# Attention with v's adds: sign turns of queries' and keys' rounded values, and the adding transfers behind them, placed 4 to 11 half-steps later

## The chip, the core and the metric

One core of a Trainium2 chip runs the whole program. The metric is device microseconds from start to end, as the median of several executions of one compiled kernel. A profile of one execution shows where its time lies.

## What is computed

Attention in which a query sees only the keys of its own hash bucket (six sign bits of a projection), then a mixture of experts on its output. Cut to what matters:

```python
q_bits = einsum('bhsd,dk->bhsk', q, proj) > 0        # k_bits likewise, 6 bits
mask   = q_bucket[:, :, :, None] == k_bucket[:, :, None, :]
scores = where(mask, q @ k.T / sqrt(D), -1e9)
attn   = exp(scores - rowmax); attn /= attn.sum(-1) + 1e-9
x      = (attn @ v) as rows of 512                    # 4 batches, 8 heads, 768 rows, 64 wide
out    = moe(x, w_gate, w1, w2)                       # 8 experts, capacity rows/8
```

Queries and keys are fp32. To multiply them with fp16 matmuls and keep fp32's precision, each is used as a rounded fp16 value and an fp16 remainder ("high" and "low").

## The kernel before, in words

Attention works on 32 heads in 8 groups of four. A head has six steps, each of two half-steps, so a group is 48 half-steps and the program lists its work by half-step. A step computes scores for one block of 128 keys (lines 322 and 323, into `pst`), ScalarE's exp (line 324, into `pt`), the rounding remainder of `pt` on GpSimd or VectorE (`lo`, lines 328 and 331), the products with v four steps later (lines 345 to 347), and about one pass that finds row maxima for a later head (lines 273 and 275). Once in 12 half-steps, so once a head, ScalarE turns a head's maxima (line 290, `mr`) and lays them into `qa` with a small DMA (line 293). These rows of line 290 are called marks below.

Group G needs its high and low parts in the layout of the matmuls (`qa`, `qb`, `ka`, `kb`, two buffers each). The road there, for G from 4 to 7, in half-steps before the group's first one (`P4`, `Z4`):

- SyncE loads `qp` and `kp` (fp32) from memory.
- ScalarE casts them to `qh` and `kh` (fp16) in eight pieces (line 149), from half-step -35 to -15.
- ScalarE writes the negative of the rounded value into `ql` and `kl` in four pieces: the sign turns (`turn`, line 153).
- GpSimd issues two adding DMAs (`adds`, line 155), each of which adds the fp32 original from memory to `ql` or `kl`, so that the remainder stands there.
- SyncE's queue then moves `qh`, `kh`, the sign bits, and last `kl` and `ql` into the matmul buffers (`moves`, lines 182 to 216), in a fixed order from half-step -47 on, that is from +1 of the group before.

`qh`, `kh`, `ql`, `kl`, `qp` and `kp` have one buffer each. So the first turn of group G writes `ql` only when the move of the group before it out of `ql` (`qb<-ql`, line 200, the last of that group's moves) has landed. Instructions of one engine run in the order in which they were written: a ScalarE instruction that waits holds every exp behind it, and the score matmuls write into three `pst` buffers that the exps must empty.

The lines that place them:

```python
def turn(G,w,p):
    A.activation(TMP[G,'l'][w][:,p],TMP[G,'h'][w][:,p],AF.Copy,scale=-1.0)
def adds(G,w):
    G_.dma_start(TMP[G,'l'][w]...,(qT,kT)[w][G]...,accum_op=ALU.add)
...
z=AP['Z3'] if G==3 else [48*(G-1)+x for x in AP['Z4']]
add(z[n],turn,G,n%2,n//2)        # n=0..3: q pair 0, k pair 0, q pair 1, k pair 1
if n<2: add(z[4+n],adds,G,n)     # q, k
```

v goes a like way inside the group before: cast (line 218), turn (line 223) and an adding DMA (`vl`, line 227) at half-step +25, and TensorE sums `vh` and `vl` at +33 (line 237).

Of the kernel before, what the change touches and what calls it, by code (L numbers as in the profile page):

```python
# [41 lines left out]
 TV=1,  # L42
 AV=[5,7],
 Z3=[77,85,88,91,93,97],
 Z4=[-31,-19,-25,-13,-19,-11],
 EA=[262, 32, 5],
 EG={2: 0, 3: 3},
 MO=['', 'AKs', 'BqL', 'lmk', 'c|ABqKLslmk', 'ABqKLs|cklm', 'ABqKLs|cklm'],
# [9 lines left out]
def attention(tc, nc, ctx, qT, kT, vv, proj, wg, x_dram, L, jp, identf, ident, B, late=None, after=None):  # L58
# [349 lines left out]
    def add(n,f,*a):  # L408
        if n>=2*(6*NH+LAG+6): raise ValueError('an operation has no step')
        at.setdefault(n,[]).append((f,a))  # L410
# [15 lines left out]
    for G in range(1,NG):  # L426
# [5 lines left out]
        for n in range(4):  # L432
            if G<3: add(p[8+n],sub,G,n%2,n//2)
            else:
                z=AP['Z3'] if G==3 else [48*(G-1)+x for x in AP['Z4']]
                add(z[n],turn,G,n%2,n//2)
# [621 lines left out]
```

## Time and profile before

| | |
|---|---|
| median of 3 runs | 742.94 us (741.41 to 744.52) |
| profiled execution | 742.8 us, of which the span is 740.9 us |
| TensorE busy in the span | 660.6 us, 89% |
| VectorE, GpSimd, ScalarE busy | 522.3, 508.9, 399.6 us |

Attention ends at about 410 us; the experts follow. Busy shares are means over stages with different limits, so the table says which engine is busiest and not what a change is worth: that is read from the stretch in which the change stands.

### The profile page before, as it was taken

Reading aid. Unit: us, or ns where it says so; the run is one execution under the profiler, and the core shown is the slowest. Engines: PE = TensorE matmul, PEld = TensorE weight load, DVE = VectorE, ACT = ScalarE, POOL = GpSimd, SP = SyncE. Lnnn points to the kernel's source line nnn. Section 1 sums busy time; section 2 is a strip of 40 time slices with the busy share of each in tenths; the row PEclk is TensorE's granted clock in tenths of the full one; section 3 lists DMA queues with packets and bytes.
Section 4 is the critical chain, followed back from the end, with each engine's and each line's share of the span. In section 5 each row is a group of like instructions: output and inputs, shape, how many; then the busy total and the mean of one; then the engine's idle time right before and its main releaser. Section 6 shows DMA issues by size and latency. Waiting matters only on the chain. (4 is left out here: it accounts for less than half of the span.)

```text
span 740.9 us, 19022 instructions
## 1 busy us (share of the span) xinstructions
PE 660.6 (89%) x7761; PEld 424.5 (57%) x7769; DVE 522.3 (70%) x1220; ACT 399.6 (54%) x821; POOL 508.9 (69%) x469
## 2 busy tenths in 40 slices
PE   8999999499589598699999669999999999999994
PEld 2666666277357366467777556555555555555551
DVE  7879889178388387389788774989878888843120
ACT  6876886467557556657557125443434344444530
POOL 7899987378558577476884054585787878797761
PEclk9999999699899899899999759999999999999998
DMA  8649778668685686676322153526170708072601
GB/s 214 195 112 198 178 180 165 135 107 175 137 145 141 131 153 162 117 159 144 33 52 66 32 157 115 191 108 237 77 282 31 282 33 284 31 284 88 239 30 42
DMA packets 65020, 104.51 MB, mean 141 GB/s; under 512 B 29040, under 2 KB 53668, under 8 KB 62884
## 3 DMA queue, kind: packets, MB, share of 16 engines
q1 hardware_dynamic: 55236, 51.10, 29.1%
q0 software_dynamic: 8944, 52.04, 24.9%
q8 instruction: 61, 1.00, 0.6%
q10 hardware_dynamic: 752, 0.15, 0.1%
q14 instruction: 27, 0.22, 0.1%
HBM read 71.32 MB, written 12.58 MB: 113 GB/s over the span
## 5 line engine op out<-in xcount | busy, mean ns | idle before, releaser
L328 POOL TENSOR_TENSOR lo<-pt 128x768 f16<-128x768 f32 x148 | 243.0, 1675 | 95.0 <-ACT pt L324 90.5
L275 DVE TENSOR_REDUCE m<-pss 128x1 f16<-128x770 f32 x192 | 181.4, 956 | 81.0 <-PE pss L273 79.9
L324 ACT ACTIVATE pt<-pst 128x384 f32<-128x384 f32 x384 | 172.4, 490 | 88.4 <-PE pst L323 81.3
L322 PE MATMUL pst<-qa,ka 128*128 128x384 f16 x384 | 127.6, 333 | 39.6 <-ACT pt L324 36.4
L345 PE MATMUL psv<-vh,pt 128*128 128x65 f16 x1152 | 126.9, 196 | 1.6 <-DVE X L363 1.6
L323 PE MATMUL pst<-qb,kb 128*128 128x384 f16 x384 | 127.5, 333 | 0.0
L347 PE MATMUL psv<-vh,lo 128*128 128x65 f16 x1152 | 126.6, 196 | 0.7 <-POOL lo L328 0.5
L346 PE MATMUL psv<-vl,pt 128*128 128x64 f16 x1152 | 126.8, 195 | 0.0
L345 PEld LDWEIGHTS <-pt 128*128 128x128 bf16 x1152 | 108.7, 99 | 18.9 <-issue 4.5
L346 PEld LDWEIGHTS <-pt 128*128 128x128 bf16 x1152 | 107.5, 100 | 11.8 <-issue 1.2
L347 PEld LDWEIGHTS <-lo 128*128 128x128 f16 x1152 | 107.4, 99 | 1.1 <-POOL lo L328 0.8
L875 ACT CAST wh<-wf 128x1024 f16<-128x1024 f32 x64 | 65.4, 1042 | 75.2 <-DMA wf<-in_w_dram,zwidx 46.6
L273 PE MATMUL pss<-ka,qa 128*128 128x385 f16 x384 | 96.2, 335 | 6.5 <-DVE m L275 5.6
L887 POOL TENSOR_TENSOR wl<-wf,wh 128x512 bf16<-128x512 f32 x74 | 84.1, 1152 | 0.0
L323 PEld LDWEIGHTS <-kb 128*128 128x128 f16 x384 | 37.9, 99 | 61.8 <-issue 41.4
L910 PEld LDWEIGHTS <-wh 128*128 128x128 f16 x544 | 50.7, 99 | 31.1 <-issue 1.4
L866 POOL DMA_INDIRECT wf<-in_w_dram,zwidx x20 | 19.6, 981 | 57.2 <-DVE zmi L799 30.6
L910 PE MATMUL ph<-xx,wh 128*128 128x384 f16 (+1 forms) x304 | 57.3, 315 | 0.3 <-issue 0.3
L922 PEld LDWEIGHTS <-hh 128*128 128x128 f16 x384 | 35.5, 98 | 36.3
L322 PEld LDWEIGHTS <-ka 128*128 128x128 f16 x384 | 38.2, 99 | 27.2 <-issue 2.8
L910 PE MATMUL po<-xx,wh 128*128 128x384 f16 x240 | 48.1, 326 | 0.0
L997 POOL TENSOR_TENSOR wl<-wf,wh 128x512 bf16<-128x512 f32 x36 | 42.6, 1211 | 4.4 <-ACT wh L875 4.3
(294 smaller groups left out, 1221.7 us busy)
## 6 DMA issues: line engine op xcount, KB each, us to landing
vp<-in_vv_dram SPq DMA_DIRECT2D x8, 768.0 KB
x_dram<-XS SPq DMA_DIRECT2D x16, 384.0 KB
qp<-in_qT_dram SPq DMA_DIRECT2D x7, 768.0 KB
kp<-in_kT_dram SPq DMA_DIRECT2D x7, 768.0 KB
qa<-qh SPq DMA_DIRECT2D x14, 192.0 KB
ka<-kh SPq DMA_DIRECT2D x14, 192.0 KB
qb<-qh SPq DMA_DIRECT2D x14, 192.0 KB
kb<-kh SPq DMA_DIRECT2D x14, 192.0 KB
```

Of the source, the lines that this page charges most:

```text
L273: T.matmul(ps[:,hf,0:HK],QA[u][:,j,qc*128:qc*128+128],KA[u][:,j,hf*HK:hf*HK+HK],start=True,stop=True)
L275: V.tensor_reduce(M6[h][:,qc:qc+1],ps[:,:,0:HK],axis=AX.XY,op=ALU.max,negate=True)
L322: T.matmul(ps[:,0:384],KA[u][:,j,kr],QA[u][:,j,r],start=True,stop=False)
L323: T.matmul(ps[:,0:384],KB[u][:,j,kr],QB[u][:,j,r],start=False,stop=True)
L324: A.activation(PT[h,kc][0][:,r],ps[:,0:384],AF.Exp,scale=0.125)
L328: eng.tensor_tensor(l,p,p.bitcast(BF)[:,1::2],op=ALU.subtract)
L345: T.matmul(av[:,c,:],ph[:,r],VH[u][:,j,kc,:],start=(kc==0 and c==0),stop=False,skip_group_check=True)
L346: T.matmul(av[:,c,0:64],ph[:,r],VL[u][:,j,kc,:],start=False,stop=False,skip_group_check=True)
L347: T.matmul(av[:,c,:],l[:,r],VH[u][:,j,kc,:],start=False,stop=False,skip_group_check=True)
L875: s.nc.scalar.copy(h[:,r],f[:,r])
L887: for _ in range(n): s.nc.gpsimd.tensor_tensor(*s.pend.pop(0)[1],op=ALU.subtract)
L910: T.matmul(p[:,r],a[:,o:o+128],b[:,d,r],start=n==0 and not c,stop=n==11 and c in (None,2),skip_group_check=c is not None)
```

## The change

One row of the table of positions: for groups 4 to 7 the turns move from half-steps -31, -19, -25, -13 (q pair 0, k pair 0, q pair 1, k pair 1) to -20, -12, -18, -9, the adds of q from -19 to -15 and those of k from -11 to -6. Group 3 has its own row, `Z3`, which stays. Nothing is computed that was not computed before.

```diff
- Z4=[-31,-19,-25,-13,-19,-11],
+ Z4=[-20,-12,-18,-9,-15,-6],
```

On ScalarE, ahead of group 5 and right behind the casts of v, this stood before (`vl` and `vh` are v's low and high parts, line 324 is the exp):

```order
L218 CAST vh_215<-vp 128x6x64
L153 ACTIVATE ql<-qh 128x768
L324 ACTIVATE pt<-pst 128x384
L223 ACTIVATE vl_216<-vp 128x384
L218 CAST vh_215<-vp 128x6x64
L324 ACTIVATE pt<-pst 128x384
L223 ACTIVATE vl_216<-vp 128x384
L149 CAST qh<-qp 128x384
L324 ACTIVATE pt<-pst 128x384 x2
L149 CAST qh<-qp 128x384
L324 ACTIVATE pt<-pst 128x384 x2
L153 ACTIVATE ql<-qh 128x768
```

Now both turns of q stand behind the next mark, and the first meets `qb<-ql` there:

```order
L149 CAST kh<-kp 128x384
L324 ACTIVATE pt<-pst 128x384
L290 ACTIVATE mr<-pst,mb_198,ms_199 24x128
L324 ACTIVATE pt<-pst 128x384
L149 CAST kh<-kp 128x384
L293 DMA qa_171<-mr 4x6x128
L324 ACTIVATE pt<-pst 128x384
L153 ACTIVATE ql<-qh 128x768
L324 ACTIVATE pt<-pst 128x384 x2
L153 ACTIVATE ql<-qh 128x768
```

The first turn has gone from ahead of the casts of q's second pair to behind two casts of k; the mark, the casts and the exps keep their order.

On GpSimd, which issues the adds between its `lo` instructions (line 328), the same stretch read before:

```order
L227 DMA vl_216<-in_vv_dram 128x1536
L558 IOTA wt_88 128x8
L328 TENSOR_TENSOR lo<-pt 128x768 x2
L155 DMA ql<-in_qT_dram 128x1536
L585 TENSOR_SCALAR wt<-wt_88 128x8
L586 TENSOR_SCALAR wtb<-wt_88 128x8
L328 TENSOR_TENSOR lo<-pt 128x768 x2
L155 DMA kl<-in_kT_dram 128x1536
```

and reads now:

```order
L227 DMA vl_216<-in_vv_dram 128x1536
L558 IOTA wt_88 128x8
L328 TENSOR_TENSOR lo<-pt 128x768 x2
L585 TENSOR_SCALAR wt<-wt_88 128x8
L155 DMA ql<-in_qT_dram 128x1536
L586 TENSOR_SCALAR wtb<-wt_88 128x8
L328 TENSOR_TENSOR lo<-pt 128x768 x2
L562 MEMSET tiny 128x1
L328 TENSOR_TENSOR lo<-pt 128x768 x2
L155 DMA kl<-in_kT_dram 128x1536
```

The add of q passes one small instruction, the add of k two `lo` and one small one. SyncE's and TensorE's orders are as before.

## Rows read from the trace of the kernel before

**Rows 1.** The page: busy us, share of the span, instructions of each engine.
```profile
PE 660.6 (89%) x7761; PEld 424.5 (57%) x7769; DVE 522.3 (70%) x1220; ACT 399.6 (54%) x821; POOL 508.9 (69%) x469
```

**Rows 2.** Waits (us in total, times, longest), 140:340, then whole span.
```profile
PE pst L322 <- ACT pt L324: 35.8, 4, 10.3
...
ACT ql L153 <- DMA qb<-ql: 31.3, 4, 8.7
```

**Rows 3.** ScalarE's timeline at the four waits: start, us, [idle <-releaser].
```profile
139.56 0.84 ACT L153 ACTIVATE ql<-qh 128x768 f16<-128x768 f16 x1 [8.73 <-DMA qb<-ql]
...
193.37 0.84 ACT L153 ACTIVATE ql<-qh 128x768 f16<-128x768 f16 x1 [7.65 <-DMA qb<-ql]
...
248.58 0.84 ACT L153 ACTIVATE ql<-qh 128x768 f16<-128x768 f16 x1 [7.30 <-DMA qb<-ql]
...
302.40 0.84 ACT L153 ACTIVATE ql<-qh 128x768 f16<-128x768 f16 x1 [7.63 <-DMA qb<-ql]
```

**Rows 4.** TensorE's timeline at the second wait, same columns.
```profile
194.64 0.48 PE L322 MATMUL pst<-qa,ka 128*128 128x384 f16 x1 [8.62 <-ACT pt L324]
...
196.86 0.53 PE L322 MATMUL pst<-qa,ka 128*128 128x384 f16 x1
...
198.95 0.33 PE L322 MATMUL pst<-qa,ka 128*128 128x384 f16 x1
```

**Rows 5.** SyncE's timeline at the second wait.
```profile
184.85 0.45 SPq L78 DMA_DIRECT2D kp<-in_kT_dram  x1
...
187.62 1.76 SPq L200 DMA_DIRECT2D qb<-ql  x2
```

**Rows 6.** Busy time by stretch: one burst, then mark to mark (L290).
```profile
core 0: us, PE busy (x) PEld busy (x) DVE busy (x) ACT busy (x) POOL busy (x), PEclk, DMA share, GB/s
185.00:195.00 10.00, 1.39 (x9) 0.68 (x7) 2.44 (x5) 2.35 (x6) 1.86 (x3) 0.81 1.00 237
125.72:148.81 23.09, 12.42 (x154) 8.43 (x150) 8.01 (x12) 11.87 (x28) 10.83 (x11) 0.70 0.60 116
181.64:201.39 19.75, 11.13 (x157) 7.83 (x154) 8.60 (x12) 11.82 (x28) 10.70 (x12) 0.83 0.52 125
237.06:256.30 19.24, 10.84 (x157) 7.74 (x154) 8.59 (x12) 11.73 (x29) 10.28 (x11) 0.82 0.59 126
290.75:310.52 19.77, 11.23 (x157) 7.85 (x154) 7.77 (x12) 11.77 (x29) 9.57 (x11) 0.83 0.59 124
343.00:352.90 9.90, 9.56 (x157) 6.94 (x154) 9.80 (x13) 8.54 (x23) 6.98 (x5) 1.00 0.74 163
201.39:212.70 11.31, 10.78 (x162) 8.01 (x159) 8.82 (x13) 9.15 (x22) 9.07 (x10) 1.00 0.83 141
160.70:172.25 11.55, 11.37 (x176) 7.49 (x174) 9.57 (x16) 5.69 (x15) 11.07 (x10) 1.00 0.93 152
212.70:227.68 14.98, 12.83 (x176) 8.52 (x174) 12.67 (x14) 5.98 (x18) 9.25 (x7) 0.89 0.66 120
```

**Rows 7.** DMA issues: 384 KB adds, median us to landing.
```profile
ql<-in_qT_dram POOLq DMA_DIRECT2D x5, 384.0 KB, 8.8
...
vl<-in_vv_dram POOLq DMA_DIRECT2D x5, 384.0 KB, 6.4
```

**Rows 8.** GpSimd's timeline: adds of k, group 3, then 4.
```profile
111.51 1.21 POOL L155 DMA_DIRECT2D kl<-in_kT_dram  x1
...
161.15 0.86 POOL L155 DMA_DIRECT2D kl<-in_kT_dram  x1
```

**Rows 9.** DMA queue of the adds, 160 to 168 us: share of 16 engines.
```profile
q0 software_dynamic: 144, 0.39, 47.4%
```

**Rows 10.** Waits for DMAs, 100 to 420 us: total, times, longest.
```profile
PE pst L237 <- DMA vl<-in_vv_dram: 1.6, 3, 0.7
...
ACT qh L149 <- DMA qp<-in_qT_dram: 0.3, 1, 0.3
```

**Rows 11.** VectorE's line 373: min/median/max ns.
```profile
L373 DVE TENSOR_TENSOR XS<-X,XS x15: 944/1350/4867, 58.2 to 402.5; 128x768 f16<-128x768 f32 x15
```

## What the change will do, predicted from the trace of the kernel before

> **What bounds the kernel now.** I read the page first: TensorE is busy 89% of the span [rows 1], so time is won only where TensorE stands still. Next the waits of TensorE through the attention of the later groups: from 140 to 340 us it waited four times for an exp of line 324, 35.8 us together, the longest 10.3 us [rows 2]. Over the whole span ScalarE waited four times for the transfer `qb<-ql` ahead of line 153, 31.3 us [rows 2]. The reader is to see that these are the same four stops. ScalarE's timeline has them: turns at 139.56, 193.37, 248.58 and 302.40 us, after 8.73, 7.65, 7.30 and 7.63 us of waiting [rows 3]. TensorE's timeline shows what the second costs: it stood for 8.62 us, a moment longer than ScalarE, since the exps have to start again first, and then a score matmul took 0.53 us where 0.33 us is usual [rows 4], for the granted clock had fallen. So the place of the turn, and not an engine's work, makes these four holes.
>
> How much they cost together is read best with the marks (line 290, one in 12 half-steps) as a ruler. The four stretches that hold a stop last 23.09, 19.75, 19.24 and 19.77 us, 81.9 us together; the same stretch of the last group, which has no turns, lasts 9.90 us, with TensorE busy 9.56 us and the clock at 1.00 throughout [rows 6].
>
> **The change, part by part.** *The first turn leaves the stalled place.* It stood 3 half-steps behind a mark and now stands 14 behind it, 2 behind the next one. What is left in the four stretches? TensorE's pattern needs 9.9 us. ScalarE was busy 11.73 to 11.87 us in them [rows 6]; two turns of 0.84 us each [rows 3] are gone from there, so 10.1 us stay, just above TensorE's pace. I take 10.4 us, because such tight neighbours lose a little to each other: 4 x 10.4 = 41.6, a gain of 40.3 us. Bounds: 42.3 us at 9.9 us each, 37.5 us at 11.1 us (one more us than ScalarE's work). This gain holds the lost clock too, since the stretches are measured whole.
>
> *Where the turns go.* The next stretch had two turns and will have three: ScalarE goes from 9.15 to 10.0 us of 11.31 us. The fourth turn goes into the stretch after it, where ScalarE is busy 5.69 us of 11.55 us [rows 6]. TensorE's own work covers both; I count 0. Without that cover the four displaced 0.84 us in two stretches of each group would cost up to 6.7 us. One turn now stands ahead of the small DMA that lays maxima for a head 9 half-steps later, 0.84 us of delay against some 8 us: nothing.
>
> *A new wait at the new place.* The transfer doesn't depend on ScalarE's progress: SyncE issued `qb<-ql` from 187.62 us on, while ScalarE was standing [rows 5]. So it lands where it landed, counted from the mark ahead, at which the stretch of [rows 6] begins: turn 139.56 - 125.72 = 13.8 us at the first stop, 193.37 - 181.64 = 11.7 us at the second, 11.5 and 11.6 us at the others [rows 3, 6]. The new turn comes 14 half-steps after that mark, at 10.4 x 14/12 = 12.1 us. The first group still waits 1.7 us, the others not at all. TensorE loses about one us more than ScalarE waits (8.62 against 7.65 [rows 3, 4]): 2.7 us. Two casts of `kh` come just ahead; `kp` is issued ahead of `qb<-ql` [rows 5] and so should land no later, which makes any wait there a part of this one.
>
> *The add of k.* It moves 5 half-steps nearer to the burst in which SyncE moves `qh`, loads `qp` and moves `kh`. From 160 to 168 us, the add's own queue takes 47.4% of the 16 engines, 3.8 us of all of them [rows 9]; that work leaves a quiet place and joins a busy one. Can it make the moves late? The trace has the case: group 3's add of k was issued at 111.51 us, right at its moves, where group 4's was at 161.15 us [rows 8], and the transfer behind group 3's moves is the one that landed 13.8 us after its mark and not 11.7. So adds that stand close cost up to 2.1 us of landing. Both of group 3's stand close, here only one does, so I take half: landing 12.7 us, a wait of 0.6 us at 12.1, and with the restart some 1.0 us in three groups, 3.0 us (0 to 2.7 each). The add of q moves into a place between SyncE's bursts: 0. GpSimd holds its `lo` instructions behind an add only if the turn is late; the turns stand 3 half-steps ahead of their adds: 0.
>
> The Trainium skill ("DMA: Bandwidth & Descriptors", Queues, rings and completion order) says that a DMA engine takes turns between the queues that have work for it, packet by packet, so the add would take its share out of the burst and not wait behind it. If all 3.8 us of it came on top of the landing, the wait at the new turn would be 15.5 - 12.1 = 3.4 us in three groups, and the total 10 us worse than with the value taken; only the uncontended neighbours in the trace speak against so much.
>
> *The add of v.* It isn't moved in the program, but the stop used to end before it: now GpSimd issues it while the transfers of 185 to 195 us run, in which the DMA engines are busy through (share 1.00 [rows 6]). Alone it lands in 6.4 us; the add of q, which meets a load, takes 8.8 us [rows 7]. TensorE waits for v's add at line 237 three times even now, 1.6 us [rows 10], so there is no slack: 0 to 2.4 us each; I take the middle, 1.2 us, four times 4.8 us.
>
> *VectorE's line 373* takes 0.94 to 4.87 us [rows 11]; the long one lies in the stretch of 14.98 us, where its neighbour has 11.55 us [rows 6]. It is an encounter with GpSimd's instructions, and moving the add of k deals these cards again: 0 on the whole, 3.4 us either way for one.
>
> Sum: -40.3 + 2.7 + 3.0 + 4.8 = -29.8 us. The profiled execution took 742.8 us (span 740.9 and 1.9 around it), 0.1 us from the median of 742.94 us, so **713 us** is forecast for the median.
>
> **The rivals.**
> - *Clean:* nothing waits anew. For it: landing at 11.7 and turn at 12.1 us. Against it: the first group, and line 237 that waits already. 742.8 - 40.3 to 42.3, some 701 to 703 us.
> - *The waits form again, shorter:* the add of k delays the burst by its whole 3.8 us or by 2.1 us, the cast of `qh` waits for `qp` as it did once for 0.3 us [rows 10], the clock falls after each of these stops too. Each group would give back 5 to 8 us: 40.3 - 4 x 5 to 8 leaves 8 to 20 us, some 723 to 735 us. Against it: no row shows landing later than 13.8 us. It is the case that the Trainium skill's turn-taking (same page and section) would bring about, if the add's whole share came out of the burst; so far the trace bears out about half of it.
> - *The stop only moves:* if the transfer were tied to ScalarE, it would slip with it and the time stay at 743 us. SyncE's rows [rows 5] speak against it.
> - *Slower:* SyncE's `kb<-kl` waits for the add of k, and `qb<-ql`, transposes and v's load stand behind it in the same queue. If that add landed so late that `qb<-ql` came over 10 us later, the new wait would exceed the old one. The add is issued some 5 half-steps later, at about 165.5 us by the old clock, and would have to land after 195 us to do this, 30 us after issue; adds take 6.4 to 8.8 us [rows 7]. At 35 us it would be four times 5 us, 763 us.
>
> **How the numbers follow.** Chances: forecast (704 to 721 us) 0.58; clean (below 704) 0.16; waits again (721 to 736) 0.18; stop only moved 0.05; slower 0.03. The range leaves out half of the clean case's lower edge, the last two cases and the upper part of the third: 700 to 727 us. Less than 0.5% (3.7 us) can't be told from no change. Faster by more: 0.58 + 0.16 + 0.18 and a little of the fourth, 0.93; within: 0.04; slower: 0.03.
>
> **What would show it.** Right: the row `ACT ql L153 <- DMA qb<-ql` falls from 31.3 us to under 6, TensorE's waits of line 322 for exps from 35.8 us to under 10; the four stretches from mark to mark last 10 to 11 us with the clock at 1.00; line 237 waits 3 to 7 us for v's add. Wrong: stretches of 13 us or more (the turn or the casts wait again), longer stretches behind the second mark (the displaced turns are not covered), landing of `qb<-ql` over 14 us behind its mark (the add of k costs more than taken), or more long rows at line 373.

## The result, and the profile after

The changed kernel took 723.67 us in the median (719.88 to 732.37) where the kernel before took 742.17 us beside it: ratio 0.973, 95% interval 0.968 to 0.978. So the change gains 2.7%, about 20 us; 30 us had been forecast (713 us, with 700 to 727 us as the range). The profiled execution of the changed kernel took 719.88 us. Of its page, the line that answers to [rows 1]:

```profile
PE 657.0 (92%) x7761; PEld 421.7 (59%) x7769; DVE 525.3 (73%) x1220; ACT 398.6 (56%) x821; POOL 509.7 (71%) x469
```

TensorE's busy share rose from 89% to 92% with the same work. The waits from 100 to 375 us for TensorE, and below them two rows of the whole span (engine, line, releaser: us in total, times, longest):

```profile
PE psv L345 <- DVE X L363: 5.7, 5, 1.6
PE pst L237 <- DMA vl<-in_vv_dram: 5.0, 3, 2.6
PE pst L322 <- ACT pt L324: 3.8, 11, 0.7
PE pst L402 <- DMA XT<-XS: 2.9, 1, 2.9
...
POOL ql L155 <- ACT ql L153: 6.2, 4, 2.0
...
ACT ql L153 <- DMA qb<-ql: 0.3, 1, 0.3
```

The four stops are gone: ScalarE waits 0.3 us for `qb<-ql` where it waited 31.3 us, TensorE 3.8 us for exps where it waited some 36 us [rows 2]. Three waits of TensorE have grown beside that: for v's adding DMA at line 237 (5.0 us, before 1.6), for a quotient at line 345 (5.7 us, before 1.4), and once for a transpose at line 402 (2.9 us, before none).

The same ruler as in [rows 6], busy time from mark to mark; the first four rows are the stretches that held the stops, the next four those that follow them, the last four the ones behind these:

```profile
125.72:136.50 10.78, 9.72 (x157) 7.01 (x154) 7.76 (x12) 10.14 (x26) 8.75 (x9) 1.00 0.84 159
175.45:185.92 10.47, 9.87 (x157) 6.92 (x154) 8.59 (x12) 10.07 (x26) 10.00 (x10) 1.00 0.81 164
224.81:236.27 11.46, 10.71 (x170) 7.46 (x167) 8.95 (x13) 10.13 (x28) 10.86 (x11) 1.00 0.81 155
270.38:280.86 10.48, 9.71 (x157) 7.01 (x154) 8.08 (x12) 9.97 (x27) 9.46 (x9) 1.00 0.80 170
136.50:153.06 16.56, 13.52 (x210) 10.13 (x207) 9.17 (x14) 10.11 (x22) 8.72 (x11) 0.90 0.84 141
185.92:202.77 16.85, 13.64 (x162) 9.58 (x159) 8.93 (x13) 10.01 (x22) 8.81 (x11) 0.80 0.69 138
236.27:247.82 11.55, 11.22 (x192) 8.69 (x192) 8.96 (x13) 10.27 (x24) 7.72 (x7) 1.00 0.92 198
280.86:295.47 14.61, 12.49 (x162) 8.88 (x159) 8.93 (x13) 9.94 (x22) 7.72 (x8) 0.88 0.75 156
153.06:166.06 13.00, 11.43 (x176) 7.54 (x175) 11.58 (x16) 6.40 (x17) 11.00 (x8) 1.00 0.74 137
202.77:215.41 12.64, 11.41 (x176) 7.52 (x175) 10.98 (x14) 6.61 (x18) 10.94 (x8) 1.00 0.76 134
247.82:260.43 12.61, 11.28 (x175) 7.46 (x174) 11.00 (x14) 6.34 (x17) 10.96 (x10) 1.00 0.75 141
295.47:308.16 12.69, 11.42 (x176) 7.54 (x175) 11.09 (x14) 6.29 (x15) 10.99 (x8) 1.00 0.75 137
```

The reader is to compare three sums. The stopped stretches: 43.2 us, before 81.9 us, a gain of 38.7 us. Those behind them: 59.6 us, and before (11.93, 11.31, 11.96 and 11.32 us by the marks) 46.5 us, a loss of 13.1 us. Those behind these: 50.9 us, and before (11.51, 14.98, 11.77 and 11.77 us) 50.0 us. The last mark came at 394.4 us and comes at 368.9 us, 25.4 us earlier. From it to the end of the span were 346.5 us and are 348.9 us; the profiles of the first five runs below have 344.7 to 345.4 us there, the unaltered changed kernel among them (345.0), so these 2.4 us belong to that execution and not to the change.

What happened in the stretch of 16.85 us? GpSimd's issue of v's add, TensorE's timeline at the sums of v (start, length, [idle before <-releaser]), and below them the stretches of 2 us around the stand (the third number from the right is the granted clock):

```profile
185.52 0.88 POOL L227 DMA_DIRECT2D vl<-in_vv_dram  x1
...
191.03 0.27 PE L237 MATMUL pst<-vh,on 128*128 128x256 f16 x1 [0.38 <-ACT pt L324]
193.95 0.37 PE L237 MATMUL pst<-vl,on 128*128 128x256 f16 x1 [2.65 <-DMA vl<-in_vv_dram]
...
196.03 0.42 PE L237 MATMUL pst<-vl,on 128*128 128x256 f16 x1
...
197.25 0.83 PE L273 MATMUL pss<-ka,qa 128*128 128x385 f16 x2
```

```profile
192.00:194.00 2.00, 0.05 (x1) 0.05 (x1) 0.84 (x1) 0.15 (x1) 1.92 (x2) 0.74 1.12 360
194.00:196.00 2.00, 2.00 (x10) 1.42 (x10) 0.00 (x0) 0.00 (x0) 0.44 (x1) 0.50 0.94 132
196.00:198.00 2.00, 2.00 (x24) 1.56 (x22) 0.49 (x1) 0.88 (x2) 0.00 (x0) 0.50 0.47 61
198.00:200.00 2.00, 2.00 (x24) 1.33 (x23) 1.12 (x2) 1.09 (x3) 0.03 (x1) 0.55 0.00 0
```

It stood for 2.65 us for `vl`, and then the granted clock lay at 0.50, the lower of its two levels, until nearly 200 us: a sum took 0.42 us instead of 0.27, a pass for maxima 0.83 instead of 0.49. The stand cost 2.65 us, and the clock, by an estimate from these rows, some 3 us more: TensorE was busy throughout the six us that followed, at half its pace. The stretch of 14.61 us holds such a stand of 1.56 us at the same line. The stretch of 16.56 us is another case: there line 237 waits for no add, and the wait is that of 2.9 us for the transpose at line 402.

And in the stretches behind? VectorE's line 175, and GpSimd's timeline beside it:

```profile
207.07 1.69 DVE L175 TENSOR_SCALAR bt<-bt 128x768 f16<-128x768 f16 x1
```

```profile
206.14 0.88 POOL L155 DMA_DIRECT2D kl<-in_kT_dram  x1
206.77 1.76 POOL L328 TENSOR_TENSOR lo<-pt 128x768 f16<-128x768 f32 x1
```

Line 175 takes 0.36 us when it is undisturbed. Here it takes 1.69 us: it starts where the issue of the add of k ends (207.02 us), and it ends 0.2 us after GpSimd's next `lo` (206.77 to 208.53 us). The other three groups show the same, 1.74 to 1.79 us. The quotients behind it on VectorE come later, and that is TensorE's wait at line 345, 1.2 to 1.6 us in each of the four groups. So the row's length goes with the `lo` beside it, which the add's new place put there: in the kernel before, a row of 0.94 us with no add near it ended 0.2 us after a `lo` too. Whether the issue has a share of its own these runs don't show. It is an encounter in time and not a fixed price: in the first experiment below, with the add of k at the same half-step, the row takes 0.63 us at most, and in four of the others one of these rows takes 4.9 us (shown at the half-way turn).

### The profile page after: what moved, and what is told of

The parts are those of the page before. It is cut to its first block, busy times and chain, and to the rows that moved or that the text cites. A ratio compares the mean times of both kernels' runs of the same rounds, so it can differ in the third digit from the quotient of the medians.

```text
span 717.8 us, 19026 instructions
## 1 busy us (share of the span) xinstructions
PE 657.0 (92%) x7761; PEld 421.7 (59%) x7769; DVE 525.3 (73%) x1220; ACT 398.6 (56%) x821; POOL 509.7 (71%) x469
## 5 line engine op out<-in xcount | busy, mean ns | idle before, releaser
L322 PE MATMUL pst<-qa,ka 128*128 128x384 f16 x384 | 125.7, 328 | 7.2 <-ACT pt L324 3.8
L323 PE MATMUL pst<-qb,kb 128*128 128x384 f16 x384 | 125.6, 327 | 0.0
L273 PE MATMUL pss<-ka,qa 128*128 128x385 f16 x384 | 94.6, 330 | 5.7 <-DVE m L275 3.1
```

Source lines behind the costliest of these rows:

```text
L273: T.matmul(ps[:,hf,0:HK],QA[u][:,j,qc*128:qc*128+128],KA[u][:,j,hf*HK:hf*HK+HK],start=True,stop=True)
L322: T.matmul(ps[:,0:384],KA[u][:,j,kr],QA[u][:,j,r],start=True,stop=False)
L323: T.matmul(ps[:,0:384],KB[u][:,j,kr],QB[u][:,j,r],start=False,stop=True)
```

## The experiments

Theory A: what the changed kernel lost again, it lost at line 237, where v's add lands late, and by the clock that falls after the stand. Theory B, the rival: it lost it to the add of k and to the turns that were moved into these stretches. All ratios are to the kernel before, run on the same chip.

**Sums of v later, on the changed kernel.**

```diff
- P3=[..., 97, 111, 1, 4, 128, ...]   P4=[..., 8, 3, 1, 4, 33, ...]
+ P3=[..., 97, 111, 1, 4, 136, ...]   P4=[..., 8, 3, 1, 4, 40, ...]
```

> The changed kernel, with TensorE's sums of v (line 237) 7 to 8 half-steps later. Theory A (v's add): in the changed kernel the stretch behind the second mark lost its time at line 237, where TensorE stood up to 2.6 us for v's adding DMA and the granted clock then fell to 0.50. Then TensorE's wait at line 237 for the DMA falls from 5.0 us to under 1, the clock stays at 1.00 in the second and fourth group's stretch, these go from 16.9 and 14.6 us to 12 to 13, and the time is 7 to 11 us under the changed kernel's, 713 to 717 us. Theory B (the add of k and the displaced turns): the stretches stay at 14 to 17 us and the time within 3 us of the changed kernel's.

**The same edit on the kernel before**, as a control.

> The kernel before, with the same later sums of v. Both theories: the sums waited only 0.9 us there in these groups, so 741 to 743 us. If it gains 5 us or more, a gain of the later sums on the changed kernel says nothing of a wait that the change made, and theory A falls.

Measured: 699.62 us on the changed kernel, ratio 0.945 (0.940 to 0.949); 737.1 us on the kernel before, ratio 0.996 (0.993 to 0.998). The stretches behind the second mark, first of the changed kernel with later sums, then of the kernel before with them:

```profile
139.91:150.51 10.60, 10.42 (x198) 8.00 (x195) 8.50 (x13) 9.53 (x21) 8.34 (x9) 1.00 1.01 214
183.56:193.40 9.84, 9.31 (x149) 6.76 (x146) 8.51 (x13) 9.20 (x21) 8.44 (x9) 1.00 1.08 217
226.27:237.01 10.74, 10.56 (x199) 8.07 (x196) 8.64 (x13) 9.82 (x23) 8.47 (x9) 1.00 0.98 212
270.36:280.19 9.83, 9.30 (x149) 6.74 (x146) 8.50 (x13) 9.19 (x22) 7.64 (x8) 1.00 1.03 223
```

```profile
146.47:157.05 10.58, 10.49 (x198) 8.05 (x195) 8.48 (x13) 8.78 (x20) 7.03 (x7) 1.00 0.82 143
198.57:207.95 9.38, 9.29 (x150) 6.85 (x147) 8.09 (x12) 8.69 (x21) 8.09 (x9) 1.00 0.90 159
251.60:262.23 10.63, 10.54 (x199) 8.06 (x196) 8.54 (x13) 8.97 (x22) 6.92 (x6) 1.00 0.82 146
306.94:316.31 9.37, 9.28 (x150) 6.84 (x147) 8.09 (x12) 8.68 (x20) 6.89 (x5) 1.00 0.96 167
```

No wait for v's add is left in either and the clock is at 1.00 in these stretches. On the changed kernel these four stretches fell from 59.6 to 41.0 us, 18.6 us; on the kernel before from 46.5 to 40.0 us, 6.6 us, which the stretches behind gave back in part (52.1 us for 50.0). So the sums cost something at their old place in either kernel, but by these profiles some 12 us of what the changed one lost there were the change's own. The control gained 3 us against the kernel run beside it, under the 5 us that would have ended theory A, though more than the expectation had. Theory A holds, with more at stake than expected (7 to 11 us; the last mark came 16.1 us earlier); theory B's number, under 3 us, is far off. Not all of the 16.1 us are line 237's: the wait for the transpose at line 402 is gone here too (6.0 us of the 18.6 lie in its stretch), and TensorE's waits at line 345 fell from 5.7 to 1.1 us, since line 175 met a `lo` only near its end.

**The turns and the add of k back at their old places.**

```diff
- Z4=[-20,-12,-18,-9,-15,-6],
+ Z4=[-20,-19,-18,-13,-15,-11],
```

> The changed kernel, with the turns and the adding DMA of k back at their old half-steps (-19, -13, -11) and those of q at the new ones. Theory A: line 237 waits as in the changed kernel, the stretches behind the second mark stay within 1.5 us of theirs; only line 175 on VectorE, 1.69 us beside the add of k, gets short again and gives back about 1 us in each of four groups: 3 to 5 us under the changed kernel, 718 to 721 us. Theory B: landing of the last move comes 1 to 2 us earlier behind its mark, the stretches behind the second mark fall by 3 us or more each, 9 to 14 us under the changed kernel.

Measured: 712.44 us, ratio 0.959 (0.952 to 0.967). TensorE's wait for v's add from 100 to 375 us, then the four stretches behind the second mark and three of those behind the third:

```profile
PE pst L237 <- DMA vl<-in_vv_dram: 8.4, 5, 2.8
```

```profile
136.86:149.62 12.76, 12.03 (x210) 9.22 (x207) 8.68 (x14) 10.63 (x23) 8.39 (x9) 1.00 0.98 179
180.99:194.64 13.65, 10.93 (x162) 8.00 (x159) 8.91 (x13) 10.52 (x23) 9.60 (x12) 1.00 0.81 165
230.23:246.19 15.96, 13.58 (x211) 10.18 (x208) 9.23 (x14) 10.82 (x26) 9.50 (x10) 0.89 0.68 144
279.39:293.65 14.26, 10.94 (x162) 8.00 (x159) 8.91 (x13) 10.52 (x24) 8.61 (x9) 1.00 0.79 164
149.62:161.12 11.50, 11.32 (x176) 7.49 (x174) 9.52 (x16) 5.66 (x15) 11.03 (x10) 1.00 0.84 157
246.19:257.94 11.75, 11.29 (x175) 7.47 (x174) 10.18 (x14) 5.71 (x16) 10.12 (x9) 1.00 0.86 160
293.65:305.40 11.75, 11.34 (x176) 7.48 (x174) 10.19 (x14) 5.55 (x15) 10.07 (x7) 1.00 0.82 160
```

The wait at line 237 stayed, 8.4 us in five: the add of k does not make v's add late. The time is another matter: 712.44 us is 11 us under the changed kernel's 723.67 us, where theory A had 3 to 5 us and theory B 9 to 14 us (by the ratios, 0.959 against 0.973 and, measured again below, 0.966, it is 5 to 10 us). The stretches do not decide it alone: two of the four behind the second mark are over 3 us shorter than the changed kernel's first profile (12.76 for 16.56 and 13.65 for 16.85 us), one is 4.4 us longer and one 0.4 us shorter, 56.6 us for 59.6 together. The changed kernel's second profile, below, has 12.30, 17.75, 15.66 and 15.50 us there, so single stretches differ by 4 us with no edit at all, with the wait for the transpose, the size of the wait for v and the fall of the clock. What speaks against theory B is the wait at line 237, which did not fall. Behind the third mark the stretches went back from 13.00, 12.61 and 12.69 us to 11.50, 11.75 and 11.75 us: the late add of k costs 0.9 to 1.5 us in these groups, at line 175, and TensorE's waits at line 345 fell from 5.7 to 1.4 us. The fourth of them was 15.07 us, with VectorE's long row at line 373 again, as in the 14.98 us of [rows 6]. The last mark came 3.1 us earlier than in the changed kernel.

**The first turn half way.**

```diff
- Z4=[-20,-12,-18,-9,-15,-6],
+ Z4=[-26,-12,-18,-9,-15,-6],
```

> The changed kernel, with the first turn of q at half-step -26, between its old place (-31) and its new one (-20). If the wait is the landing time less the time at which the program comes to the turn, it is 11.6 - 8 x 0.87 = 4.7 us in three groups and some 6.5 us in the first, 18 to 21 us together where the kernel before had 31.3 us and the changed one 0.3; TensorE loses that and about 2 us more each with the restart and the clock, less what line 237 no longer waits: 733 to 738 us. If only the order (ahead of the casts or behind them) counted, it would be as the kernel before or as the changed one.

Measured: 733.15 us, ratio 0.988 (0.983 to 0.992). ScalarE's wait from 100 to 375 us, the first two stretches, and the first one behind the third mark with VectorE's and GpSimd's timelines in it:

```profile
ACT ql L153 <- DMA qb<-ql: 14.6, 4, 4.0
```

```profile
130.18:144.91 14.73, 10.34 (x151) 7.04 (x148) 8.00 (x12) 10.74 (x28) 9.13 (x9) 0.93 0.83 160
185.40:199.99 14.59, 10.50 (x151) 6.95 (x148) 8.84 (x12) 10.59 (x28) 9.58 (x9) 0.91 0.81 168
...
157.61:176.01 18.40, 13.43 (x176) 8.78 (x175) 15.24 (x16) 6.61 (x16) 11.52 (x10) 0.81 0.57 113
```

```profile
162.13 4.93 DVE L175 TENSOR_SCALAR bt<-bt 128x768 f16<-128x768 f16 x1
```

```profile
161.63 0.87 POOL L155 DMA_DIRECT2D kl<-in_kT_dram  x1
162.25 4.59 POOL L328 TENSOR_TENSOR lo<-pt 128x768 f16<-128x768 f32 x3
```

14.6 us in four waits, 3.7 us each: less than 4.7 us, but between none and 7.8 us. The turns start 12.1, 11.9, 12.3 and 11.7 us behind their marks, where the kernel before had 13.8, 11.7, 11.5 and 11.6: in the last three groups the landing keeps its time behind the mark to within 0.8 us while the turn moves by 5 half-steps (in the first it comes 1.7 us sooner). The four stretches (14.93 and 14.32 us are the others) lie between 10.5 and 20 us. It is the position in time that counts, not the order of the turn and the casts. TensorE's wait for v's add is 0.5 us here: with half of the stop in place, v's add is hidden again.

That the time fell into the range of 733 to 738 us is in part luck. The reckoning had nothing for line 175, and in the first group that row took 4.93 us here: it started during the issue of the add of k and ended 0.2 us after three `lo` in a row. TensorE stood 5.0 us for the quotient behind it, the clock fell, and the stretch took 18.40 us where the changed kernel's first profile has 13.00 us. The profiles of the three runs that follow show the same row and 17.87 to 18.41 us there. So the profile of 719.88 us had met the mild form of this encounter.

**The changed kernel again, v's load left out, and v's add earlier** (one chip, side by side):

> The changed kernel, unaltered, as the base of the runs beside it. All theories: a ratio of 0.97 to 0.98. The last mark should come at 367 to 371 us; from it to the end before took 346.5 us, the changed kernel's first profile 348.9 us: if this run has 345 to 346 us, the 2.4 us more belong to that execution and not to the change.

```diff
-   LD[G]=(..., dp.tile([128,4,6,64],F32,name="vp",bufs=1))
+   LD[G]=(..., LD[3][2] if G>3 else dp.tile([128,4,6,64],F32,name="vp",bufs=1))
    def load(G,w):
      if w==0: alloc_load(G)
+     if w==2 and G>3: return
```

> The changed kernel without the loads of vp for groups 4 to 7 (v's high parts there are those of group 3, so the output is not the reference's; everything else runs). Theory A1: v's adding DMA lands late because it shares the DMA engines with this load, which SyncE issues 2 us behind it; then TensorE's wait at line 237 falls from 5.0 us to under 1.5 and the second and fourth group's stretch from 16.9 and 14.6 us to 11.5 to 12.5: 8 to 10 us of attention less. Theory A2: it is late because of the transposes and moves ahead of it; then the wait stays over 3 us and the gain is under 4 us. Rival B (less DMA work helps everywhere): the first and third stretch shrink too.

```diff
- AV=[5,7],
+ AV=[5,4],
```

> The changed kernel, with v's adding DMA for groups 4 to 7 at half-step +22 instead of +25, so issued some 2.6 us earlier. Theory A1 (the load behind it delays it): most of the add is over when the load begins, the wait at line 237 shrinks by about the 2.6 us, to nearly 0, 5 to 8 us of attention less. Theory A2 (the transfers ahead delay it): it meets more of them and lands at nearly the same time, under 2 us less.

Measured: the changed kernel 719.17 us, ratio 0.966 (0.960 to 0.972), single executions from 712 to 728 us; in the profiled one, which took 727.78 us, the last stretch, from the last mark to the end, was 345.0 us, as expected. The last mark came at 380.8 us and not at 367 to 371 us: of the 12 us against the first profile, 4.9 us lie behind the third marks (the row of 4.9 us again, four stretches of 55.8 us for 50.9), 4.8 us ahead of the first stop, and TensorE waited 8.6 us in five at line 237. Without v's load 718.37 us, ratio 0.962 (0.956 to 0.969); with v's add earlier 719.85 us, ratio 0.968 (0.964 to 0.973). Neither differs from the changed kernel beside it by more than the intervals. The wait at the sums without the load, from 110 to 330 us (line 238 there, since the edit adds a line):

```profile
PE pst L238 <- DMA vl<-in_vv_dram: 4.6, 3, 2.1
```

In the same window the changed kernel's two profiles have 4.2 and 8.2 us, so a wait remains without the load, over the 3 us that theory A2 asked for. The four stretches behind the second mark took 55.0 us, 4.6 to 6.2 us less than in those two profiles, which lies between the two theories (A2 had under 4, A1 8 to 10 us). The load behind the add can be a part of the delay, but not all of it. That the rest is due to the transfers ahead (SyncE's `kp`, `kl`, `ql` and the transposes) is argued and not shown: none of them was taken away by itself. The earlier issue gained nothing either, and in its profiled execution (727.73 us) it did not help where it should: in the second group the add, issued at 192.71 us, released TensorE only at 206.81 us, and TensorE waited 6.9 us for transposes at line 402. So of the edits tried, none on the side of the add took the wait away; the later sums did.

**Later sums and the old places of k together.**

```diff
- Z4=[-20,-12,-18,-9,-15,-6],   P3 ... 128   P4 ... 33
+ Z4=[-20,-19,-18,-13,-15,-11], P3 ... 136   P4 ... 40
```

> The changed kernel with the later sums of v and the k turns and adds at their old half-steps together. If the two costs are separate (line 237's wait with the clock behind it, and line 175 beside the add of k), the gains add: the stretches behind the second mark at 10 to 11 us as with the later sums alone, those behind the third at 11.7 to 12 us where they are 12.8 to 13.2 us, 3 to 5 us under the later sums alone, a ratio of 0.938 to 0.942. If line 373 meets GpSimd's three instructions again as it did with the old place, one stretch is 3 us longer and the two are equal. Rival: they fall out on the same waits and the sum is no better than the later sums alone.

Measured: 701.58 us, ratio 0.946 (0.942 to 0.950), the same as the later sums alone. The four stretches behind the third mark:

```profile
151.35:164.21 12.86, 12.67 (x188) 8.64 (x186) 9.73 (x17) 6.14 (x16) 10.45 (x10) 1.00 0.81 153
193.94:206.64 12.70, 12.70 (x188) 8.73 (x187) 9.07 (x14) 6.43 (x18) 10.43 (x10) 1.00 0.77 147
237.38:251.43 14.05, 12.79 (x187) 8.70 (x186) 12.65 (x15) 6.17 (x16) 11.18 (x11) 1.00 0.70 136
282.28:294.98 12.70, 12.70 (x188) 8.73 (x187) 8.97 (x14) 6.10 (x15) 10.12 (x8) 1.00 0.81 156
```

The rival was right: with the later sums alone these four last 13.18, 12.91, 12.76 and 12.76 us, and they stay at 12.7 to 14.1 us (in the one of 14.05 us line 373 takes 4.5 us). The sums now stand there themselves and TensorE is busy through in two of the four, so the old place of k has next to nothing left to give. The best version of those run is thus the changed kernel with the later sums, 5.5% under the kernel before.

## Why the prediction held, and where it was off

*The stops and their size.* Right. They went, and the four stretches gave 38.7 us of the 40.3 forecast; the third of them kept 1.2 us, a cast of `kh` that waited for `kp`. The half-way turn confirms the reckoning that the transfer lands at a fixed time behind the mark. One thing in the description of the kernel before is to be set right for this: the half-steps of casts, turns and adds count from the first one of the group before (the program's `48*(G-1)+x`), as the +1 of the moves does. So, for groups 5 to 7, the turn at -31 came 16 half-steps behind the first of the moves of the group before it, the last of which it waits for, and at -20 it comes 27 behind.

*The new wait at the new place* (2.7 us) came to 0.3 us, and *the add of k* (3.0 us, by a later landing of `qb<-ql`) didn't show there at all: the turns of the last three groups found the transfer landed. The case that the prediction read from the trace does not bear it out: it put the landing at 13.8 us in the first group down to group 3's adds, but with the same adds the kernel before with later sums has its first turn 11.4 us behind the mark. (By the prediction's own rule of one us of restart on top of the wait, the term would have been 1.6 us a group and not 1.0.) The term was not far off in size and wrong in mechanism. The late add of k costs 0.9 to 1.5 us per group by VectorE's line 175, and over 6 us in one group in four of the profiles; I had named no one there. The Trainium skill ("GPSIMD Engine Reference", Specifications) says that GpSimd shares its SBUF interface with VectorE and that instructions of VectorE in a two-port mode or with two SBUF inputs contend with it; the row of 1.69 us beside a `lo`, against 0.36 us, fits that. Line 175 has one tensor input, so it would have to be the two-port mode; no run here shows in which mode it runs.

*The displaced turns* (0). The prediction named longer stretches behind the second mark as the sign that these turns are not covered. The stretches did get longer, but not for that: with later sums and the turns at the same places they last 9.83 to 10.74 us. *GpSimd behind the turns* (0): it did wait for the turn ahead of the add of q, 6.2 us in four times, but TensorE waited only 0.4 us for a `lo` of GpSimd in the whole run.

*The add of v* is the step that was furthest off, by its size: 1.2 us a group, 4.8 us in all. The wait itself was 5.0 us, as taken (0.75 us of it in the last group's stretch, after these four). But I counted the wait alone, though I had read from [rows 4] that the clock falls behind a stand of TensorE. The two stretches in which line 237 stood 2.65 and 1.56 us lost 5.5 and 3.3 us, 8.8 us with the clock. Of the 13.1 us lost behind the second mark the other 4.6 us lie in the first group, with the wait for a transpose that I had not counted (the third stretch gained 0.4 us). In the sum, 5.4 us of the two terms above that did not come hid most of this: that part of the forecast held by luck. The median, 10.7 us above the forecast, lies where the rival of shorter waits had put it (723 to 735 us); neither a late burst nor a cast of `qh` brought it there, but its other point, a clock that falls after new stands, came true at line 237.

So the profiled execution, 22.9 us faster than the one before, misses the 29.8 us in these parts: 1.6 us at the stops, 2.6 us behind the second mark (13.1 us for the 10.5 of the three terms), 0.9 us behind the third (the late add of k cost more than that, but VectorE's long row of [rows 6] fell out), and 2.4 us at the end that are not the change's, less 0.6 us gained elsewhere. The median lies 3.8 us above this execution.

What stays open: why the clock fell after a stand of 1.6 us in one stretch (0.88 on the mean of 280.86 to 295.47) and not after 2.2 and 2.8 us in two others (the stretches of 13.65 and 14.26 us, at 1.00), and when VectorE's rows of lines 175 and 373 have to sit out three `lo` in a row. Single executions of the changed kernel differ by 12 to 15 us on a chip, those with the later sums by 3 to 5 us. In the two profiles of the changed kernel 4.9 of 12 us are line 175's encounter and what follows it; that the later sums quiet the rest was not tested by itself.

## What to carry to other kernels

An instruction that waits for a transfer, on an engine that runs in program order, can be moved by a ruler in the program: count the landing from a mark that recurs and put the instruction behind it; here that was worth 38.7 us and could be reckoned to 1.6 us. Then ask who was hidden by the stop. A transfer that used to be issued after it now runs amid the burst that caused it, and whoever uses its result has lost time to hide it: look for a wait that was already a few tenths of a us long (line 237) and move its user too. Price a stand of TensorE with the clock that it may bring, not by its length alone. And profile the same kernel twice before you read a single stretch: here single stretches differed by 4 to 5 us with no edit.

## What was unexpected of the hardware

The granted clock fell to 0.50 during a stand of 2.65 us and stayed there for 6 us of full work, so that the stand cost about twice its length. A VectorE instruction of 0.36 us lasted 1.69 us beside one GpSimd `lo` and 4.93 us beside three in a row, and ended 0.2 us after them each time. In the kernel before, v's adding DMA landed 6.4 us after issue in the median; issued at 185.52 us into the burst it released TensorE only at 193.95 us, 8.4 us later, and issuing it earlier brought no time.
